# Four VectorE additions put ahead of ScalarE copies in the second MLP stage, with the order of all turns written anew

## The chip, the cores and the metric

The kernel runs on one core of a Trainium2 chip. The metric is the device time of one execution in microseconds (us). The core has five engines with queues of their own: PE (TensorE, matrix products, with its weight loads shown apart as PEld), DVE (VectorE), ACT (ScalarE), POOL (GpSimd) and SP (SyncE), which issues nearly all DMAs here. Each engine works through its own instructions in the order of the program and stops at the first one whose operands or buffers are not ready.

## The reference

```python
def _attn_ref(q, k, v, alpha):            # (B, H, S, D) = (4, 8, 768, 48)
    for t in range(S):
        state = alpha[:, :, t, :, None] * state + einsum('bhd,bhe->bhde', k[:, :, t], v[:, :, t])
        y[:, :, t] = einsum('bhd,bhde->bhe', q[:, :, t], state)

def _moe_ref(x, g_ln, w_ch1, w_ch2):      # x: (4, 768, 384), w_ch1: (384, 1536), w_ch2: (1536, 384)
    xn = (x - mean(x)) / sqrt(var(x) + 1e-06) * g_ln
    return x + maximum(xn @ w_ch1, 0.0) @ w_ch2
```

The output of the first function, its heads laid side by side, is the x of the second. The two weights arrive as float64 and are rounded to float32 inside the kernel.

## The kernel before

**Tiling.** The 768 positions are cut into six chunks of 128, and a unit of attention is one chunk of one of the four batches. Such a unit takes logarithms of alpha (L260), sums them with a triangular matrix (L474), scales q and k (L279), has them turned by DMA (L310, L313, L317; the first two chunks on TensorE, L295), forms scores (L490, masked by L343), the update of the state (L359, L372, L374), the output (L399), a layer norm and the transposed, normalised x (L463), which lands in the tile xT.

**MLP.** Chunk 0 uses plain products (L513, L525). Chunks 1 to 5 use a fast scheme with fewer products: x is combined by additions on VectorE (L775), fifteen hidden products (L801) are made for each of two groups of rows, their PSUM results are added up by VectorE, ScalarE and GpSimd (L809 to L844), relu runs on ScalarE (L852), the hidden values are combined on VectorE (L611), and twenty products (L624, `product`) give the output. In `product` each result `acc` lies in one PSUM bank and is added to one or two of the outputs `o(k)` (L634, L637) or kept: for n = 15, 11, 14 and 4 ScalarE copies it to e, f, g and q4 (L643, L648, L671, L684) and VectorE adds it to an output as well. `late` runs on GpSimd (L640).

**Buffers.** PSUM has eight banks in one ring (tag "bank"). Turned q and k, x combinations, hidden combinations and intermediate results share eleven SBUF tiles (tag "sum"). A new tile takes the one that was given back first, and its first writer waits for the last reader of the old content.

**Order.** Nothing is scheduled by a planner at build time. Each part of the work is a Python generator, a turn runs it to its next `yield`, and the string `ORDER` names the 1566 turns one by one. Lower case letters a to x are the 24 units of attention (a to d chunk 0, e to h chunk 1, and so on to u to x chunk 5); 0, 1, 2 and 3 are loads of alpha, k, q and v; 4 the sums of logarithms for two units, 5 the scores for two units; A to L rounding of the weights; Y, Z, P, Q the MLP of chunk 0; S and W weight combinations; X the combinations of x; M the products of chunks 1 to 5 (an even turn is a matrix product, the odd turn after it what is done with the result); V the hidden products of chunk 5; N the hidden combinations; R the relus; O reloads of x. Below, M190 is the turn of M with index 190, X22 the turn of X with index 22, and w0 the first turn of unit w; indices begin at 0. A turn's place is its index in `ORDER`. All instructions are issued in this order, each to the queue of its engine.

Of the kernel before, what the change touches and what calls it, by code (L numbers as in the profile page):

```python
# [20 lines left out]
STAGED = 3  # L21

ORDER = (
    "00aa00212b1cd2aab2b3cda1cabaadb0babb1aabbabBbccabccdedfacddaaaadd4acBfbbbb1dbbd2"
    "ecaAbff3ecffffdeeaeAee5bBdA0dgAccdhCdcdc1B4dYgYdYcccd2eCYYYYe3ghACggcgcghYhhhhdc"
    "ZBCf3ZZgfhZCeDDfe5fhYYD0YEZZ3eFEiYeZZY1gDYffjh2EYeYEFhfF4eFeffYgj0hjGigYYYjjYiiG"
    "ZgGZZhGjYiiZZZZHIjHYH3iHIj1SZZZZilZIZZkZSjJPh4ZgfjhgJiSiJ3g2SSgghKghgQSSSPlSSSSS"
    "SSeePKhYl5ISfKjjgjlkejSeShkSeklllPlfS3gLkjSSkkijLkLWQWWWWQQWifegffSSlgklfkihhhhh"
    "gejf0hjQj0iij31PQii23SPP5llnSkkii0PXXXiQMmX4Mmlk2XXXX1nlXMjkXlkMnniMM30MWMMMXMMM"
    "MMMMMMQMM2p1MnmOMRklMMnMmnWjoMMiMi4k3kmpllpnl0lW0mkmlpMMMmMMn1MMMWqMnMRjMMMRRRMM"  # L30
    "MMMMMMMm2MrRMmMMlMR2MMoj0ii5mnnkmmlORRnion3WmjRMMMlknMMROMWmknmNNNNmM4mkkkmlmNRM"
    "njNnpMMM11MMnlOo3j33MrMnkqlNNNNNN2MoNoMMMMpMoMMWMmoMMNXXnXMMNONXMqmmMMMMMMMMMMqX"
    "nXXXXqqoMMtMMmMXXMMnMppoMMMMMMMMMMMpRp0MnMMMMMMMMMMMq0vqM5pppoRooroqRrrpprrrM1OM"
    "MMMpMMpM1MRoMMoMMMRMoM2oMpqpMprMoMMrMMMsMMMMMROn5qrqR0RRmqqorrp4or3sMnMqq2rusorr"
    "RqRMMMprMtNRqOoNNNqNNotrmNMMMMMsssoNrMrMMNMMMNNpprNMMoppMMttMqMp0MMMnrsr2rrMNMNN"
    "3NM0tMt1MOMsw3MMXMXXXX1XMXMXMMqMXsMMMMtMM2tsXMMMMMMMMXMMMMMMMMMMMMMtRMMMM5tRttts"
    "4uMtxssMuMMMMRRMMMMvvq1ssquMMROMrMMMMMqussMRvuvM42sMttRtRtutM3tMtMMMqsMMRMMMMMMM"
    "sNtttMN3uOvxRtRNNNs1MNMRtMMMMMxONNNNssxqMMssNNMMvNMMMxsMMMMMMNMvNMxxNXMXXXXXOMMM"
    "MMMMMMXXXXx2XOwuMMMMMMMMMMMMMMMMMMMMMMMMMMRuvvRM3MMMRMRxM5uuuvuuvvwwwwwwMMRvOMMM"
    "MMMMMMMvMMvMxwuMwMuMvMMvMMMMMMMOuuvuRuRRvv5RxwxwxvvxwMMwMwRMNMMRRuMwvxwuxuNNNwxw"  # L40
    "wwxxwxNMwNxNNNvMMxxMMMMxNwNMMMMMMMMMMxXXMXXXXXXXXNMMXMMMVMVVVNVVVVVVVVVVVVVVVVVV"
    "VVVVVVVVVVVVVVVVVVVVVNVRRRRVVVONVVRVVRVVVVNVVVMVMMMMMOMMMMMMMVOORRRNNNNMMMMMMRRR"
    "NNNNNMMMMMNNNNMMMMMMMMMMMMMMMMMNNNMMMMMMMMMMMM"
)


# [1 line left out]
def kernel(  # L48
# [454 lines left out]
    def send(c, b, cols=slice(0, DM)):  # L503
        nc.sync.dma_start(out[b, c * P:(c + 1) * P, cols], ob_of[c, b][:, cols])
# [53 lines left out]
    def weights_ready():  # L558

        if "b" not in win:  # L560
            b = {(t, h): w2[:, t * NT:(t + 1) * NT, h * HM:(h + 1) * HM]
                 for t in range(3) for h in range(2)}
            win["b"] = {4: b[2, 0], 7: b[0, 1], 11: b[2, 0], 14: b[1, 0], 15: b[1, 0], 17: b[0, 0]}
        return win["b"]
# [23 lines left out]
    def blocks_of(c):  # L588
        if c not in win:
            win[c] = a = [third_of(c, t, b // HB)[:, :, b % HB] for b in range(B) for t in range(3)]  # L590
            win["a", c] = {1: a[10], 3: a[0], 4: a[8], 10: a[3], 14: a[7], 16: a[9], 17: a[6],
                           18: a[5]}
        return win[c], win["a", c]
# [23 lines left out]
    def product(c, n):  # L617
        if n == SECOND[0]:
            u = [work.tile([P, 512], FP32, name="u", tag="sum", bufs=11) for i in range(3)]
            win["u"] = [u[i // 2][:, i % 2 * HM:][:, :HM] for i in range(5)]  # L620
        acc = ps.tile([P, HM], FP32, name="ops", tag="bank", bufs=8)
        lhs, rhs = blocks_of(c)[1][n], weights_ready()[n]
        for j in range(NT):
            nc.tensor.matmul(acc, lhs[:, j], rhs[:, j], start=(j == 0), stop=(j == NT - 1))  # L624
        yield
        e, f, g, q4, r8 = win["u"]

        def o(k):
            return ob_of[c, k // 2][:, k % 2 * HM:][:, :HM]

        copy = nc.scalar.copy

        def add(x):
            nc.vector.tensor_add(x, acc, x)  # L634

        def sub(x):
            nc.vector.tensor_sub(x, x, acc)  # L637

        def late(x, y, op="add"):
            getattr(nc.gpsimd, f"tensor_{op}")(x, x, y)  # L640

        if n == 15:
            copy(out=e, in_=acc)  # L643
            add(o(0))
        elif n == 3:
            add(o(0))
        elif n == 11:
            copy(out=f, in_=acc)  # L648
            sub(o(0))
        elif n == 2:  # L650
            nc.vector.tensor_sub(f, acc, f)
        elif n == 18:
            sub(o(1))
            sub(o(3))
        elif n == 10:
            add(o(2))
        elif n == 19:
            sub(o(3))
            add(o(5))
        elif n == 0:  # L660
            add(e)
        elif n == 1:
            sub(o(1))
            sub(o(7))
        elif n == 6:
            sub(o(1))
            late(o(1), e)
            late(o(1), f)
            send(c, 0)
        elif n == 14:  # L670
            copy(out=g, in_=acc)  # L671
            add(o(4))
        elif n == 5:
            nc.vector.tensor_sub(g, acc, g)
            late(f, g)
        elif n == 9:
            sub(f)
            late(o(2), f)
            late(o(3), f)
            send(c, 1)  # L680
        elif n == 8:
            nc.vector.tensor_add(r8, acc, e)
        elif n == 4:
            copy(out=q4, in_=acc)  # L684
            add(o(4))
        elif n == 17:
            add(o(4))
        elif n == 12:
            sub(o(5))
            add(o(7))  # L690
        elif n == 13:
            add(q4)
            late(o(5), q4)
            late(o(5), g, "sub")
            late(r8, q4, "sub")
            late(o(7), r8)
            late(o(6), r8)
        elif n == 7:
            add(o(5))
            send(c, 2)  # L700
            send(c, 3, slice(HM, DM))
        else:
            add(o(6))
            send(c, 3, slice(0, HM))
        yield
# [154 lines left out]
    def mlp():  # L860
        for c in range(1, NCB):
            if c + 1 < NCB:
                yield from hidden_products(c)
            for n in SECOND:
                yield from product(c, n)
# [51 lines left out]
```

## Time and profile before

| | us |
|---|---|
| median of 3 runs (415.96 to 416.23) | 415.96 |
| the profiled execution | 415.94 |
| its span | 414.2 |
| PE busy (matrix products) | 401.8, 97% |
| PEld busy (weight loads) | 352.4, 85% |
| DVE busy | 325.0, 78% |
| ACT busy | 231.4, 56% |
| POOL busy | 159.4, 38% |

The granted clock of TensorE is full through the whole span. 1.7 us of the profiled execution lie outside its span. Views name an instruction by its line in the kernel and by its tiles (written<-read); the number in brackets at a row of the timeline is the idle time of the engine just before, with what ended it. SPq is SP's queue issuing a DMA; the time in such a row is the issue, not the transfer.

### The profile page before, as it was taken

How to read it: one execution, taken by the hardware profiler on the slowest of the kernel's cores; microseconds unless marked ns; L12 is line 12 of the kernel's file. 1: busy time of each engine (PE TensorE's matmuls, PEld its weight loads, DVE VectorE, ACT ScalarE, POOL GpSimd, SP SyncE). 2: the span in 40 equal slices, each digit the busy share in tenths (PEclk: the TensorE clock that was granted, in tenths of full speed). 3: DMA queues.
4: the chain of work that ended last, by engine and by line, in shares of the span. 5: the costliest groups of instructions: out<-in, count | busy, mean ns of one | idle time of the engine just before them, and what ended most of it. 6: DMA issues, size and time to landing. Idle time of an engine off the chain costs nothing.

```text
span 414.2 us, 11459 instructions
## 1 busy us (share of the span) xinstructions
PE 401.8 (97%) x4568; PEld 352.4 (85%) x4568; DVE 325.0 (78%) x622; ACT 231.4 (56%) x528; POOL 159.4 (38%) x180
## 2 busy tenths in 40 slices
PE   8979999999999999999999998999999999999996
PEld 6868878666578899988899977899988899889996
DVE  4599989999799799986688566779957677766764
ACT  6897468897158887337578113975125972142100
POOL 4250110001138660546731147641554700668214
PEclk9999999999999999999999999999999999999999
DMA  7979966989887968657765773464654742100301
GB/s 225 284 233 241 299 196 178 252 280 227 160 257 240 211 176 207 218 146 169 181 185 146 234 200 48 112 217 95 196 121 113 134 126 69 40 0 2 114 21 57
DMA packets 108061, 68.43 MB, mean 165 GB/s; under 512 B 73788, under 2 KB 100028, under 8 KB 108008
## 3 DMA queue, kind: packets, MB, share of 16 engines
q1 hardware_dynamic: 107976, 67.69, 61.1%
q8 instruction: 36, 0.59, 0.6%
q14 instruction: 17, 0.14, 0.1%
q0 software_dynamic: 32, 0.00, 0.0%
HBM read 34.29 MB, written 21.06 MB: 134 GB/s over the span
## 4 chain that ended last, share of the span: by engine, by line
PE 81%; DMA 5%; DVE 4%; SPq 3%; ACT 3%; POOL 2%; issue 1%; DVEq 0%; POOLq 0%; ACTq 0%
PE ops L624 30%; PE hps L801 28%; PE hps L513 6%; PE ops L525 6%; PE yps L399 4%; PE aps L490 2%; PE ups L359 2%; SPq L463 2%; DMA ra<-in_alpha_dram 2%; PE lps L474 1%; DMA rk<-in_k_dram 1%; DMA vn<-in_v_dram 1%; PE tps L295 1%; DMA turned<-sent 1%; PE yps L383 1%
## 5 line engine op out<-in xcount | busy, mean ns | idle before, releaser
L640 POOL TENSOR_TENSOR ob<-ob,u 128x192 f32<-128x192 f32 x40 | 26.2, 667 | 90.5 <-DVE ob L637 74.0
L801 PE MATMUL hps<-sum,w 128*128 128x256 f32 x192 | 46.9, 380 | 0.0
L852 ACT ACTIVATE hT<-hT 128x512 f32<-128x512 f32 x48 | 28.8, 624 | 23.7 <-POOL hT L823 17.8
L801 PEld LDWEIGHTS hps<-sum,w 128*128 128x128 f32 x192 | 36.3, 190 | 5.0
L624 PE MATMUL ops<-w,hT 128*128 128x192 f32 x224 | 39.8, 326 | 0.0
L374 POOL TENSOR_TENSOR mid<-mid,gate 112x192 f32<-112x192 f32 x20 | 11.4, 576 | 68.7 <-DMA gate<-row 22.4
L624 PEld LDWEIGHTS ops<-w,hT 128*128 128x128 f32 x224 | 37.0, 190 | 0.3
L801 PE MATMUL hps<-xT,w 128*128 128x256 f32 x136 | 34.6, 381 | 0.0
L513 PE MATMUL hps<-xT,w 128*128 128x256 f32 x144 | 32.6, 382 | 1.0 <-DVE mid L372 1.0
L310 ACT COPY planes<-qk 128x1024 uint16<-128x1024 uint16 x32 | 32.6, 1038 | 1.2 <-DVE qk L279 1.2
L525 PE MATMUL ops<-w,hT 128*128 128x384 f32 x96 | 32.2, 490 | 0.0
L513 PEld LDWEIGHTS hps<-xT,w 128*128 128x128 f32 x144 | 26.9, 190 | 5.7 <-DVE mid L372 1.1
L634 DVE TENSOR_TENSOR ob<-ops,ob 128x192 f32<-128x192 f32 x50 | 17.0, 350 | 15.5 <-PE ops L624 4.8
L801 PEld LDWEIGHTS hps<-xT,w 128*128 128x128 f32 x136 | 25.6, 190 | 4.1 <-DVE at L343 0.6
L624 PE MATMUL ops<-ws,sum 128*128 128x192 f32 x160 | 28.5, 326 | 0.0
L525 PEld LDWEIGHTS ops<-w,hT 128*128 128x128 f32 x96 | 17.9, 190 | 11.7
L624 PEld LDWEIGHTS ops<-ws,sum 128*128 128x128 f32 x160 | 26.4, 190 | 0.1
L260 ACT ACTIVATE la<-ra 128x384 f32<-128x384 f32 x24 | 12.2, 519 | 23.7 <-DMA ra<-in_alpha_dram 23.7
L624 PE MATMUL ops<-ws,hT 128*128 128x192 f32 x128 | 23.4, 326 | 0.0
L374 POOL TENSOR_TENSOR st<-st,gate 112x192 f32<-112x192 f32 x16 | 12.1, 765 | 25.7 <-DVE st L372 25.2
L624 PE MATMUL ops<-more,sum 128*128 128x192 f32 x120 | 22.0, 326 | 0.0
L624 PEld LDWEIGHTS ops<-ws,hT 128*128 128x128 f32 x128 | 21.3, 190 | 0.1
(253 smaller groups left out, 1096.4 us busy)
## 6 DMA issues: line engine op xcount, KB each, us to landing
ws<-in_moe_w_ch_dram SPq DMA_DIRECT2D x12, 768.0 KB
sent<-planes SPq DMA_DIRECT2D x32, 256.0 KB
vn<-in_v_dram SPq DMA_DIRECT2D x12, 384.0 KB
kept<-x SPq DMA_DIRECT2D x20, 192.0 KB
sentx<-parts SPq DMA_DIRECT2D x20, 192.0 KB
ob<-kept SPq DMA_DIRECT2D x20, 192.0 KB
out_dram<-ob SPq DMA_DIRECT2D x19, 192.0 KB
rq<-in_q_dram SPq DMA_DIRECT2D x16, 192.0 KB
```

What stands on the lines that cost most here:

```text
L260: nc.scalar.activation(out=la, in_=raws.pop(("a", c, b)), func=AFT.Ln)
L310: part(c)(out=planes, in_=natural.rearrange("t (d w) -> t w d", w=2))
L359: nc.tensor.matmul(up[h, p], qk_of(c, b)[ts, 1, p, i, :h.stop - h.start], vn[ts, i, p], start=True, stop=True)
L374: nc.gpsimd.tensor_mul(new, new, by)
L399: nc.tensor.matmul(yps[r][halves[s], i, p], of, by, start=not (odd and inner), stop=bool(inner or not odd), skip_group_check=bool(odd))
L513: nc.tensor.matmul(hps, w1[:, j // 2, f, j % 2 * P:][:, :P], xT_of[0][:, f, bs], start=(f == 0), stop=(f == NF - 1))
L525: nc.tensor.matmul(ops_of[b], hT_of[c][:, j, b], w2[:, j], start=(j == 0), stop=(j == NJ - 1))
L624: nc.tensor.matmul(acc, lhs[:, j], rhs[:, j], start=(j == 0), stop=(j == NT - 1))
L634: nc.vector.tensor_add(x, acc, x)
L640: getattr(nc.gpsimd, f"tensor_{op}")(x, x, y)
L801: nc.tensor.matmul(acc[:, i], w, b, start=True, stop=True)
L852: nc.scalar.activation(out=x, in_=x, func=AFT.Relu)
```

## The change

In `product` the order of two lines is turned in the branches for n = 15, 11, 14 and 4: VectorE's addition from `acc` is issued ahead of ScalarE's copy of `acc`, where before it came behind. Each branch runs once per chunk 1 to 5, so twenty pairs are turned. Besides, `ORDER` is another string with the same 1566 turns, each generator named equally often as before. Of the 382 turns with a matrix product, 188 have another rank among them, by 1.7 places in the mean over all.

Places in `ORDER` of the turns that are spoken of below:

| turn | what it is | before | after |
|---|---|---|---|
| B3 | last two rounding steps of a weight piece (L198, L200) | 121 | 83 |
| a20, b20 | xT of chunk 0, first two units (L452) | 97, 103 | 109, 108 |
| 5, index 0 | scores of e and f (L490) | 102 | 123 |
| Y0 | first hidden product of chunk 0 (L513) | 124 | 134 |
| 3, index 8 | load of v for the units k and l (L133) | 413 | 402 |
| g23, h24, e23, f24 | transposes of x of chunk 1 (L463) | 400, 405, 401, 403 | 416, 417, 420, 421 |
| 4, index 4; k12; l12 | sums of m and n; state updates of k and l | 443, 447, 446 | 388, 433, 440 |
| M0 | first hidden product of chunk 1 (L801) | 440 | 468 |
| w0 | logarithm for unit w (L260) | 972 | 1020 |
| M190, M191 | product n = 4 of chunk 2, its addition and copy | 974, 975 | 967, 968 |
| X22 to X29 | eight combinations of x of chunk 3 | 976 to 987 | 952 to 965 |
| t9, s9 | last DMA transposes of t and s (L317) | 1027, 1003 | 1038, 1064 |
| 5, index 7 | scores of s and t (L490) | 1033 | 1065 |
| M228, M252 | hidden products of chunk 3 | 1032, 1105 | 1033, 1062 |

```diff
--- before.py
+++ after.py
@@ -21,26 +21,26 @@
 STAGED = 3
 
 ORDER = (
-    "00aa00212b1cd2aab2b3cda1cabaadb0babb1aabbabBbccabccdedfacddaaaadd4acBfbbbb1dbbd2"
-    "ecaAbff3ecffffdeeaeAee5bBdA0dgAccdhCdcdc1B4dYgYdYcccd2eCYYYYe3ghACggcgcghYhhhhdc"
-    "ZBCf3ZZgfhZCeDDfe5fhYYD0YEZZ3eFEiYeZZY1gDYffjh2EYeYEFhfF4eFeffYgj0hjGigYYYjjYiiG"
-    "ZgGZZhGjYiiZZZZHIjHYH3iHIj1SZZZZilZIZZkZSjJPh4ZgfjhgJiSiJ3g2SSgghKghgQSSSPlSSSSS"
-    "SSeePKhYl5ISfKjjgjlkejSeShkSeklllPlfS3gLkjSSkkijLkLWQWWWWQQWifegffSSlgklfkihhhhh"
-    "gejf0hjQj0iij31PQii23SPP5llnSkkii0PXXXiQMmX4Mmlk2XXXX1nlXMjkXlkMnniMM30MWMMMXMMM"
-    "MMMMMMQMM2p1MnmOMRklMMnMmnWjoMMiMi4k3kmpllpnl0lW0mkmlpMMMmMMn1MMMWqMnMRjMMMRRRMM"
-    "MMMMMMMm2MrRMmMMlMR2MMoj0ii5mnnkmmlORRnion3WmjRMMMlknMMROMWmknmNNNNmM4mkkkmlmNRM"
-    "njNnpMMM11MMnlOo3j33MrMnkqlNNNNNN2MoNoMMMMpMoMMWMmoMMNXXnXMMNONXMqmmMMMMMMMMMMqX"
-    "nXXXXqqoMMtMMmMXXMMnMppoMMMMMMMMMMMpRp0MnMMMMMMMMMMMq0vqM5pppoRooroqRrrpprrrM1OM"
-    "MMMpMMpM1MRoMMoMMMRMoM2oMpqpMprMoMMrMMMsMMMMMROn5qrqR0RRmqqorrp4or3sMnMqq2rusorr"
-    "RqRMMMprMtNRqOoNNNqNNotrmNMMMMMsssoNrMrMMNMMMNNpprNMMoppMMttMqMp0MMMnrsr2rrMNMNN"
-    "3NM0tMt1MOMsw3MMXMXXXX1XMXMXMMqMXsMMMMtMM2tsXMMMMMMMMXMMMMMMMMMMMMMtRMMMM5tRttts"
-    "4uMtxssMuMMMMRRMMMMvvq1ssquMMROMrMMMMMqussMRvuvM42sMttRtRtutM3tMtMMMqsMMRMMMMMMM"
-    "sNtttMN3uOvxRtRNNNs1MNMRtMMMMMxONNNNssxqMMssNNMMvNMMMxsMMMMMMNMvNMxxNXMXXXXXOMMM"
-    "MMMMMMXXXXx2XOwuMMMMMMMMMMMMMMMMMMMMMMMMMMRuvvRM3MMMRMRxM5uuuvuuvvwwwwwwMMRvOMMM"
-    "MMMMMMMvMMvMxwuMwMuMvMMvMMMMMMMOuuvuRuRRvv5RxwxwxvvxwMMwMwRMNMMRRuMwvxwuxuNNNwxw"
-    "wwxxwxNMwNxNNNvMMxxMMMMxNwNMMMMMMMMMMxXXMXXXXXXXXNMMXMMMVMVVVNVVVVVVVVVVVVVVVVVV"
-    "VVVVVVVVVVVVVVVVVVVVVNVRRRRVVVONVVRVVRVVVVNVVVMVMMMMMOMMMMMMMVOORRRNNNNMMMMMMRRR"
-    "NNNNNMMMMMNNNNMMMMMMMMMMMMMMMMMNNNMMMMMMMMMMMM"
+    "0aa00bbc21021ca2bad1a0abaabdcdbbebaBaa3a2bb1ccfccbc4bccfBeaa01b2dBdacdaddgAdbhbb"
+    "3bbBeafaddf4febffdcefbaAahCebaedeAd2d3cdddA5ccgccd1C3eYfdfdc0eCYYYYCeYfYicggYYYe"
+    "cfAjhggggfB4efhef1ieeecfhDhEhhffDZ5CYZZZZDZ3ghFEZZZgYZjEZZDF2g0hhZGZghE3iFFikgYj"
+    "YgZGYiZilihijjHYYYhYYjhjGG4IhjHggZZggiHShjYIZZZkYZZYSSSSIiSSjZJQJhY32QSSSSSSIS5S"
+    "j1SijlJPjjSHejLPikegg0ghhSklQlkikkK0lik3LijlLlKlSiPPkKWQklnWmWiWWlg14feSeeeihghQ"
+    "fj3PShfh2ifff215ghnSefSkmiPlQkQiQkklSSnjlWinlOXnmmXX0XXjXnmm31XXmX0PMlkSWMMMMMXX"
+    "MMM21MMMMpM0MMMMnjljMMMkMMRMMMlWMo4mmklpllllMllpPWnknMM3MmMMMMkMp0MMMMMWMMMMRRMn"
+    "irMMMMRR3R3M2MOMoMMM0M5nmWnRRmnmnpMmmOlMkopRkMMq02nR1MNOkmMMkMM4mnkkRNijjjjmNNNN"
+    "jntnmoo1MWMMMMMiNkNollMMNMMmWRNsq2mMNNoio3MpMj0MpN0MnMMNMMMqNMrMXqMXMMMMqNMqMMnn"
+    "MqXXXXXX3XqMMMpMMMMMMoMMMMMMMXMMMMMXMMMMMMMMMMovnMpO5noo3Rp4poOrrourMrrMMooMr1MM"
+    "MMMMMMRRoORRRMMMMpotMpMpmMptMMMMMqqrnsoMprMooRMMMRpppm5r2rrqRq1ppqqMqooRRoMoNNpM"
+    "NNMMMrrMMp1mqmrtMOp2prqMmo4rNsqqNMNNRrnnrntNNMNp2MMMMMM3NMtMMMMsN1MMMMNNXMMNMXXX"
+    "MXsXXXMMMMMMMrXXsr00OMuuMMMqt3MMMMMMMMMsMXtMMMMOMMMMMMMMMrMMwM2tMqvurrrrMMMssMtM"
+    "MMMMRMMMqMMMMMMMMMMMMMMqs5sstsxsstttqtMRMMsMMuRtvRRRRROM4uuu3tssRNsNtMRttstRwsMN"
+    "MtqNMMMtN3svRMtOxqNvvsMNNNtMMMMt2NN3MMsMMNMMMMMMst1usNMMNvvMMNMMxxMMMNXXXXXMMXXX"
+    "XMMMMMM2MMMMMMXMMMMxxMXMMMMMMMMvuMMMMMMvMMMMM1M5vuRvRRuxvwwOvxuwwxwuwOMMMMMvMMMM"
+    "MuMMvRMRuwMMMMMxMw3MMMvvMuMMMuuuRMu5xwxxvuvRwwMxwwRMuMvvRMMMMRxwvRvRNNxwxuwNNwxN"
+    "vwwNNNNNNOxxxxxwOxNwNxMMMMMMMMMMMMMMMMMMwMMXXXXXXMOXXXXNMVMMMMVNNVVXVVVVVVVVVVVM"
+    "VVVVVVVVVVVVVVVVVVVVVVVVVVVVVVVVVRRRRRVVVVVVVVVVVMMRMVMMRRORRRMMMMMNNNNNNNMMNRMN"
+    "NNOMMMMMMONNMMMMMMMMMMMMMMMMMNNNMMMMMMMMMMMMMM"
 )
 
 
@@ -640,13 +640,13 @@
             getattr(nc.gpsimd, f"tensor_{op}")(x, x, y)
 
         if n == 15:
+            add(o(0))
             copy(out=e, in_=acc)
-            add(o(0))
         elif n == 3:
             add(o(0))
         elif n == 11:
+            sub(o(0))
             copy(out=f, in_=acc)
-            sub(o(0))
         elif n == 2:
             nc.vector.tensor_sub(f, acc, f)
         elif n == 18:
@@ -668,8 +668,8 @@
             late(o(1), f)
             send(c, 0)
         elif n == 14:
+            add(o(4))
             copy(out=g, in_=acc)
-            add(o(4))
         elif n == 5:
             nc.vector.tensor_sub(g, acc, g)
             late(f, g)
@@ -681,8 +681,8 @@
         elif n == 8:
             nc.vector.tensor_add(r8, acc, e)
         elif n == 4:
+            add(o(4))
             copy(out=q4, in_=acc)
-            add(o(4))
         elif n == 17:
             add(o(4))
         elif n == 12:
```

## The prediction

> **What bounds the kernel now.** The page first: the span, and the busy time of each engine.
>
> ```profile
> span 414.2 us, 11459 instructions
> PE 401.8 (97%) x4568; PEld 352.4 (85%) x4568; DVE 325.0 (78%) x622; ACT 231.4 (56%) x528; POOL 159.4 (38%) x180
> ```
>
> PE is idle for 414.2 − 401.8 = 12.4 us and no other engine is near full. The change adds and removes no instruction, so PE's 401.8 us stay as long as the clock stays, and all that can move is the 12.4 us. Where they lie is read from the windows by stage (columns: length, busy time and instructions of PE, PEld, DVE, ACT, POOL, granted clock, DMA share, GB/s).
>
> ```profile
> 0.00:30.38 30.38, 26.72 (x410) 21.26 (x410) 20.06 (x44) 25.25 (x59) 12.32 (x24) 1.00 0.80 244
> 30.38:111.54 81.16, 80.05 (x1050) 59.84 (x1046) 75.63 (x122) 57.12 (x128) 8.39 (x13) 1.00 0.88 231
> 111.54:116.28 4.74, 3.12 (x78) 2.00 (x77) 3.58 (x10) 3.19 (x10) 0.00 (x0) 1.00 0.87 271
> 116.28:235.00 118.72, 118.08 (x1461) 108.37 (x1461) 97.47 (x190) 75.47 (x174) 57.37 (x59) 1.00 0.73 192
> 235.00:256.37 21.37, 19.24 (x215) 16.33 (x213) 14.60 (x30) 4.96 (x13) 11.86 (x12) 1.00 0.67 164
> 256.37:411.00 154.63, 154.60 (x1364) 144.60 (x1364) 113.33 (x228) 65.39 (x149) 69.42 (x74) 1.00 0.35 92
> 411.00:414.24 3.24, 0.00 (x0) 0.00 (x0) 0.36 (x1) 0.00 (x0) 0.00 (x0) 1.00 0.35 121
> ```
>
> Length less PE busy gives the idle time: 3.7 in the opening, 1.1, then 1.6 in under five microseconds at the first product of chunk 1 (I call this the junction), 0.6, 2.1 around 235 to 256, nothing in the long last stretch, and a tail of 3.2 (the last output leaving), which the change doesn't touch. The clock is full in all of them. So there are three places to work out: opening, junction, and the stretch from 235 us, which I call the late place. PE's waits name what ends them (total, times, longest):
>
> ```profile
> PE xps L449 <- DVE xn L438: 1.1, 1, 1.1
> PE hps L513 <- DVE mid L372: 1.0, 1, 1.0
> ```
>
> The one of 1.1 lies in the opening, that of 1.0 at 54 us; the others of over 0.6 us stand in brackets in the timeline rows below.
>
> **The four swaps.** DVE waits for the copies in two large pieces:
>
> ```profile
> DVE ob L634 <- ACT u L684: 4.1, 1, 4.1
> DVE ob L634 <- ACT u L671: 2.5, 1, 2.5
> L684 ACT COPY u<-ops 128x192 f32<-128x192 f32 x5 | 1.6, 316 | 32.6 <-PE ops L624 32.6
> ```
>
> Copy and addition only read `acc`, yet the later one in the program waits for the earlier. Turned round, the addition waits for PE alone and ACT's copy waits for the addition. For a pair in which both engines are free this shifts the same two reads about: the addition may begin up to 316 ns earlier (row L684) and the copy later by the length of an addition, some 0.35 us. In itself that is nothing, since DVE is busy 78% and ACT 56% while PE works through eight banks ahead of them. It counts only where ACT is stuck when its copy comes up, and there the late place stands.
>
> **Late place.** The timeline:
>
> ```profile
> 235.30 0.52 ACT L260 ACTIVATE la<-ra 128x384 f32<-128x384 f32 x1 [7.25 <-DMA ra<-in_alpha_dram]
> 235.73 0.30 ACT L684 COPY u<-ops 128x192 f32<-128x192 f32 x1
> 236.06 0.36 DVE L634 TENSOR_TENSOR ob<-ops,ob 128x192 f32<-128x192 f32 x1 [4.13 <-ACT u L684]
> 239.45 1.13 PE L801 MATMUL hps<-sum,ra 128*128 128x256 f32 x4 [0.81 <-DVE sum L775]
> 245.19 6.05 SPq L317 DMA_TRANSPOSE turned<-sent  x3
> 246.70 1.24 SPq L317 DMA_TRANSPOSE turned<-sent  x1
> 247.61 2.75 PE L801 MATMUL hps<-sum,w 128*128 128x256 f32 x12
> 252.59 0.69 DVE L833 TENSOR_TENSOR hT<-hps,hT 128x512 f32<-128x512 f32 x1 [2.23 <-POOL hT L827]
> 253.65 1.10 PE L490 MATMUL aps<-turned 48*64 48x64 f32 x59 [1.30 <-DVE hT L833]
> ```
>
> The first four rows are a chain: ACT stands 7.25 us at w0, whose alpha has not landed; the copy of n = 4 (M191) is queued behind it; DVE's addition waits 4.13 us for the copy, with X22 and the other combinations of x queued behind; PE runs out of combined x and waits 0.81 us. After the change three things break it: the addition is ahead of the copy, w0 stands at place 1020 instead of 972, and X22 to X29 (eight additions of about 0.42 us, 3.4 us in all) stand ahead of M190. Any one would do, so I take the 0.81 as gone.
>
> The 1.30 us at 253.65 belong to the scores of s and t (turn 5, index 7). They are put down to DVE's L833, but that ends at 253.28 while the scores read what the DMA transposes `turned` bring, whose issue ends, in the row of three, at 245.19 + 6.05 = 251.24; start at 253.65 is 2.4 us after that. A transpose at the junction behaves alike (below: issued until 107.29 + 2.52 = 109.81, its reader starts 2.6 us later at 112.40). So the wait is a landing. After the change the scores stand 12 hidden products later; a product is four instructions of L801, 2.75 / 3 = 0.92 us by the row of twelve, so that is 11 us, far more than 1.3. But the last transposes, s9, stand at place 1064, directly ahead of the scores at 1065. Their buffer of the ring is read until M242, five products = 4.6 us ahead of the scores, while one issue (1.24) and the landing (2.4) take 3.6. That leaves 1.0 us: no wait at best, and if SP needs as long for it as for the row of three, 6.05 + 2.4 − 4.6 = 3.9. I take 0.6, the length of one or two short issues more than the margin covers; it is nearer to the row of one. Late place: −0.81 − 1.30 + 0.6 = **−1.5** (−2.1 to +1.8).
>
> **Junction.**
>
> ```profile
> 107.29 2.52 SPq L463 DMA_TRANSPOSE xT<-sentx  x1
> 109.86 1.23 SPq L120 DMA_DIRECT2D ra<-in_alpha_dram  x2
> 111.13 0.59 SPq L133 DMA_DIRECT2D vn<-in_v_dram  x1
> 111.82 0.41 SPq L116 DMA_DIRECT2D rk<-in_k_dram  x1
> 112.40 0.76 DVE L775 TENSOR_TENSOR sum<-xT 128x256 f32<-128x256 f32 x2 [2.11 <-DMA xT<-sentx]
> 112.47 1.10 PE L801 MATMUL hps<-xT,extra 128*128 128x256 f32 x4 [0.93 <-issue]
> 113.62 0.88 PE L474 MATMUL lps<-la,consts 64*64 64x384 f32 x8
> 114.91 0.42 DVE L775 TENSOR_TENSOR sum<-sum,xT 128x256 f32<-128x256 f32 x1
> 115.14 1.14 PE L359 MATMUL ups<-vn,qk 64*64 64x48 f32 x64 [0.65 <-DMA vn<-in_v_dram]
> 116.21 1.13 PE L801 MATMUL hps<-sum,ra 128*128 128x256 f32 x4
> ```
>
> M0 waits 0.93 us for the last transposed x of chunk 1 (DVE's first addition starts at 112.40 with the same landing), then k12 and l12 wait 0.65 for v. Sum 1.58. After the change the v load stands ahead of the four transposes (place 402, they at 416 to 421), and the sums (0.88) and state updates (1.14) stand ahead of M0: 2.0 us of work that covers the landing. Both waits go. What is late next is M2, which needs X0 to X6; these take DVE from 112.40 to 114.91 + 0.42 = 115.33. PE would be there at 116.21 − 1.58 = 114.6, so 0.7 us come back if the transposes land as before.
>
> They may land later. Six loads (two L120 together 1.23, L133 0.59, L116 0.41 and three more like it) now stand ahead of the last transpose on SP, 3.5 us of issue. Where SP was waiting for turned units anyhow, loads moved up fill idle time; if it had none, the landing is at 112.40 + 3.5 = 115.9, X6 ends 2.9 later with M2 at about 118.4, which is 2.2 us behind its present 116.21 and means a wait of 3.8. SP's issue ahead of 109.86 depends on `sentx`, made by other engines, so I take 0.7: **−0.9** (−1.6 to +2.2).
>
> **Opening.**
>
> ```profile
> 25.56 1.16 PE L490 MATMUL aps<-qT,kT 48*64 48x64 f32 x64 [0.76 <-ACT kT L300]
> 26.40 0.55 DVE L452 TENSOR_TENSOR xT<-xps,small 128x384 f32<-128x384 f32 x1
> 30.38 0.92 PE L513 MATMUL hps<-xT,w 128*128 128x256 f32 x3
> L198 DVE SCALAR_TENSOR_TENSOR ws<-ws 128x768 int32<-128x768 int32 x12 | 11.8, 980 | 1.4 <-ACT ws L196 1.3
> L200 DVE SCALAR_TENSOR_TENSOR w<-w,ws 128x768 f32<-128x768 f32 x12 | 12.1, 1006 | 0.4
> L196 ACT ACTIVATE ws<-ws,small 128x768 int32<-128x768 int32 x12 | 12.3, 1027 | 3.1 <-DVE ws L194 2.0 <-ACT hT L516 0.9
> L271 ACT ACTIVATE lps<-lps 128x384 f32<-128x384 f32 x24 | 11.8, 490 | 0.0
> ```
>
> B3 moves ahead of the xT of a20 and b20: 980 + 1006 ns = 2.0 us more DVE work before them. The last of these ends at 26.95 and Y0 starts at 30.38, a margin of 3.4 us that falls to 1.4, so it costs nothing; without that cover it would be 2.0. On ACT, ahead of the copies that the first scores (turn 5, index 0) read, stand in addition one L196 (1.03), two L260 (0.52 each, as at 235.30) and a pair L270, L271 (0.98): 3.05 us. The scores move from 25.56 to 28.6; their turn is moved back from place 102 to 123 to match, with Y0 ten places later. With the same work ahead of it, Y0 comes between 30.3 and, if the two engines' delays don't hide behind each other, about 32. I take **+0.3** (−0.5 to +1.7: half of the wait of 1.1 saved, or Y0 at 32). The wait of 1.0 near 55 us I leave.
>
> **All other places.** 188 of 382 matrix turns change rank in stretches that now show 0.6 us idle in 118.72. Some sums are made much earlier in the order (4, index 4: 443 to 388) and hold a PSUM bank longer. There is nearly nothing to gain here and something to lose: **+0.3** (0 to 1.5).
>
> **Sum.** −1.5 − 0.9 + 0.3 + 0.3 = −1.8 from the profiled execution's 415.94 (span 414.2 and 1.7 outside it), which is the median's 415.96 to the second digit: 414.1.
>
> **Rivals.**
>
> *SP's queue is the late one (slower).* One mechanism: loads put ahead of DMA transposes on SP delay the landing of turned data. At the junction the wait is 3.8 instead of 0.7 (+3.1); at the late place the scores keep their 1.3 instead of 0.6 (+0.7): 414.1 + 3.8 = 417.9. It decides once the moved-up loads find less than about 3 of their 3.5 us as idle time of SP. For it: DMA shares of 0.88 and 0.87 in the two windows there, the highest of the kernel. Against: the last transpose's source is made by other engines, and while SP waits for it the loads cost nothing. Chance 0.30.
>
> *The wait is only turned round (no difference).* ACT's copy now waits for the addition, and the copy of n = 4 is itself an operand of a later addition. If DVE is behind at such a place, ACT and then relu and layer norm behind it wait, and half of the 0.81 comes back (+0.4); with other places at +1.1 instead of 0.3 this is 414.1 + 0.4 + 0.8 = 415.3. The trace speaks half for it: the 4.13 us are a wait between two readers. The Trainium skill ("PSUM — Partial Sum Buffer", section "PSUM bank collisions raise a hardware error") says that any two engines at one bank and quadrant collide, two readers included, so that their accesses must be ordered; by that rule the swap cannot remove the wait, only reverse it, and the sum would be 415.3. The 4.13 us between two readers agree with the ordering. Chance 0.16.
>
> *More goes than I count.* The scores of s and t wait for nothing (−0.6), M2 neither (−0.7), and half of the 1.0 or the 1.1 in the first 55 us goes, with nothing lost elsewhere: about 412.2. Chance 0.07.
>
> **How the numbers follow.** The forecast, 414.1, has 0.47, its own range 413.0 to 415.1. Faster is forecast and gain case, 0.47 + 0.07 = 0.54; same is the turned wait, 0.16 (0.2% is 0.83 us, about what a measurement of this kernel can tell from no change); slower is SP's queue, 0.30. The range reaches from the gain case's 412.2 to SP's 417.9, which leaves out the outer halves of these two, less than 2 in 10.
>
> **What would show it.** Right: no DVE addition L634 waiting over 2 us for L684; no PE wait for `sum` near 235 us; the junction's idle time below 1 us with the wait now at M2; the scores of s and t waiting below 1 us; PE busy still 401.8. Wrong: an L801 at the start of chunk 1 waiting 2 us or more behind `sum` or `xT` (SP's queue); the opening's idle time above 5 us; several new waits of 0.5 us between 116 and 235 us or behind 256 us, in particular for banks that ACT's late copies hold.

## The result, and the profile after

The changed kernel takes 421.17 us (median of 4 runs, 420.04 to 422.76) against 416.1 us for the kernel before in the same call: a ratio of 1.012, 95% interval 1.0083 to 1.0156. It is slower by 5 us; 414.1 had been forecast, with a range up to 417.9. The profiled execution took 422.76 us. Runs of different calls come from different chips, so times below are compared by their ratio to the kernel before in the same call.

The page of the changed kernel, span and engines:

```profile
span 421.0 us, 11454 instructions
PE 405.5 (96%) x4568; PEld 355.7 (85%) x4568; DVE 326.7 (78%) x622; ACT 230.2 (55%) x528; POOL 159.1 (38%) x180
```

The span grew by 6.8 us: TensorE's idle time by 3.1 (12.4 to 15.5), and, which no term of the prediction allowed for, its busy time by 3.7 with the same 4568 instructions. The windows by stage, cut as in the prediction (Y0 starts at 33.73, M2 at 121.75; the columns are as before, with the granted clock behind POOL; the tail of 3.2 us is as before and left out):

```profile
0.00:33.73 33.73, 28.19 (x411) 23.09 (x411) 21.64 (x45) 26.05 (x63) 11.40 (x24) 0.95 0.87 259
33.73:113.00 79.27, 79.27 (x1077) 59.12 (x1077) 72.97 (x117) 58.39 (x136) 11.31 (x13) 1.00 0.82 228
113.00:121.75 8.75, 4.38 (x48) 2.79 (x46) 6.67 (x16) 3.91 (x5) 0.12 (x1) 1.00 0.95 191
121.75:126.05 4.30, 4.30 (x12) 3.53 (x13) 3.88 (x7) 0.59 (x1) 1.19 (x2) 0.60 0.88 271
126.05:240.00 113.95, 112.07 (x1429) 101.92 (x1428) 91.33 (x182) 66.51 (x154) 53.01 (x55) 1.00 0.68 172
240.00:261.00 21.00, 21.00 (x110) 19.36 (x109) 15.30 (x31) 9.75 (x23) 12.07 (x14) 1.00 0.56 163
261.00:417.80 156.80, 156.31 (x1489) 145.93 (x1487) 114.51 (x230) 64.98 (x147) 70.00 (x75) 1.00 0.40 98
```

| TensorE idle (last row: lost), us | before | after | change | forecast |
|---|---|---|---|---|
| start to junction | 3.7 + 1.1 | 5.5 + 0.0 | +0.8 | +0.3 |
| junction | 1.6 | 4.4 | +2.7 | -0.9 |
| M2 to 240 us | 0.6 | 1.9 | +1.2 | +0.3, with the row "behind it" |
| late place | 2.1 | 0.0 | -2.1 | -1.5 |
| behind it | 0.0 | 0.5 | +0.5 | |
| lost clock: 5% of 33.73 and 40% of 4.30 | 0 | 3.4 | +3.4 | none |

The late place is as clean as the better end of its range. The loss is the junction, and two stretches in which the granted clock is half. TensorE's waits name the operands:

```profile
PE hps L801 <- DVE sum L775: 4.6, 2, 4.2
PE ups L359 <- DMA vn<-in_v_dram: 2.3, 1, 2.3
```

The timeline of the junction (SP's issue, DVE, PE):

```profile
108.31 6.71 SPq L463 DMA_TRANSPOSE xT<-sentx  x4
...
117.73 0.43 DVE L775 TENSOR_TENSOR sum<-xT 128x256 f32<-128x256 f32 x1 [1.94 <-DMA xT<-sentx]
118.08 0.55 DVE L279 TENSOR_TENSOR qk<-rk,lps 128x384 f32<-128x384 f32 x1
118.54 0.55 DVE L279 TENSOR_TENSOR qk<-rq,eq 128x384 f32<-128x384 f32 x1
119.01 0.42 DVE L775 TENSOR_TENSOR sum<-xT 128x256 f32<-128x256 f32 x1
...
121.75 0.46 PE L801 MATMUL hps<-sum,ra 128*128 128x256 f32 x1 [4.16 <-DVE sum L775]
```

The four transposes of chunk 1's x stand in one row on SP and end at 115.02 (before: 109.81). The x lands at 117.73 (before: 112.40). VectorE then scales unit m between X0 and X1, 0.93 us, and M2 waits 4.16 us for X6.

What x itself waited for stands in the chain of work that ended last (first two rows: start, length, and what it was) and in SP's own waits (third row):

```profile
105.67 5.25 DMA sentx<-parts
113.74 3.97 DMA xT<-sentx
SPq L463 <- DMA sentx<-parts: 1.1, 1, 1.1
```

The writings of x to `sentx` are issued late and close together. They stand behind four transposes of `turned`, where before they alternated with them, from 94.07 on (those rows are shown in "SP's queue by itself" below):

```profile
97.53 5.44 SPq L317 DMA_TRANSPOSE turned<-sent  x4
104.12 0.95 SPq L461 DMA_DIRECT2D sentx<-parts  x2
```

The third writing, issued at 105.67, takes 5.25 us to land, and 1.1 us of the row of 6.71 is SP waiting for it. SP's row of issues that leads up to this begins 3.3 us later than before (91.83 instead of 88.58, the first writing of `planes`) and is 2.0 us longer from there to the end of the last transpose (23.2 instead of 21.2).

What the clock did is seen when the time is cut into the stretches in which it was granted (3.41 us each):

```profile
13.41:16.82 3.41, 1.54 (x24) 1.00 (x16) 0.93 (x3) 2.32 (x6) 1.22 (x2) 1.00 0.95 289
16.82:20.23 3.41, 2.87 (x56) 2.90 (x58) 2.74 (x5) 1.01 (x1) 0.00 (x0) 0.50 0.68 210
115.80:119.21 3.41, 1.78 (x7) 0.95 (x5) 1.48 (x4) 0.55 (x1) 0.00 (x0) 1.00 1.03 208
119.21:122.63 3.42, 0.89 (x4) 0.84 (x5) 3.25 (x9) 1.92 (x3) 1.00 (x2) 1.00 0.70 149
122.63:126.05 3.42, 3.42 (x10) 2.73 (x9) 3.04 (x5) 0.59 (x1) 0.31 (x1) 0.50 0.95 306
```

A stretch in which TensorE idles 1.87 us (3.41 - 1.54) or 2.53 us is followed by one at 0.50; the stretch with 1.63 us idle was not. Each costs up to 1.7 us, half its length. The Trainium skill ("TensorE: Matmul & The Clock Gate", section "Part 1: The HAM clock gate (the "warmup" mystery)") has a free-running window of 3413 ns, which these stretches agree with; it drops the clock after a whole idle window, and here half of one was enough.

### The profile page after: what moved, and what is told of

Its sections match the earlier page's. It is cut to its first block, busy times and chain, and to the rows that moved or that the text cites. A ratio compares the mean times of both kernels' runs of the same rounds, so it can differ in the third digit from the quotient of the medians.

```text
span 421.0 us, 11454 instructions
## 1 busy us (share of the span) xinstructions
PE 405.5 (96%) x4568; PEld 355.7 (85%) x4568; DVE 326.7 (78%) x622; ACT 230.2 (55%) x528; POOL 159.1 (38%) x180
## 4 chain that ended last, share of the span: by engine, by line
PE 77%; DMA 7%; ACT 7%; DVE 4%; SPq 2%; issue 2%; POOL 1%; ACTq 0%; POOLq 0%; DVEq 0%
PE hps L801 30%; PE ops L624 29%; PE hps L513 8%; PE yps L399 4%; DMA sentx<-parts 2%; PE ups L359 2%; PE aps L490 2%; DMA vn<-in_v_dram 2%; DVE sum L775 1%; PE ops L525 1%; PE lps L474 1%; DMA xT<-sentx 1%; DMA ra<-in_alpha_dram 1%; DMA kept<-x 1%; ACT xn L432 1%
## 5 line engine op out<-in xcount | busy, mean ns | idle before, releaser
L801 PE MATMUL hps<-sum,w 128*128 128x256 f32 x192 | 47.9, 385 | 0.0
L801 PEld LDWEIGHTS hps<-sum,w 128*128 128x128 f32 x192 | 36.9, 193 | 5.2
L801 PE MATMUL hps<-xT,w 128*128 128x256 f32 x136 | 34.6, 381 | 0.0
L513 PE MATMUL hps<-xT,w 128*128 128x256 f32 x144 | 32.7, 382 | 0.3 <-DVE w L200 0.3
L513 PEld LDWEIGHTS hps<-xT,w 128*128 128x128 f32 x144 | 26.8, 190 | 4.0 <-PE yps L383 0.4
L801 PEld LDWEIGHTS hps<-xT,w 128*128 128x128 f32 x136 | 25.6, 190 | 3.5
L685 ACT COPY u<-ops 128x192 f32<-128x192 f32 x5 | 1.6, 319 | 44.6 <-DVE ob L634 44.6
L820 POOL TENSOR_TENSOR hT<-hT,u 128x512 f32<-128x512 f32 x8 | 10.3, 1289 | 35.6 <-DVE u L819 35.6
L624 PEld LDWEIGHTS ops<-ws,hT 128*128 128x128 f32 x128 | 21.2, 190 | 0.0
```

Of the source, the lines that this page charges most:

```text
L513: nc.tensor.matmul(hps, w1[:, j // 2, f, j % 2 * P:][:, :P], xT_of[0][:, f, bs], start=(f == 0), stop=(f == NF - 1))
L801: nc.tensor.matmul(acc[:, i], w, b, start=True, stop=True)
L820: add_late(c4, c4, u2)
```

## Experiments

Turns are moved in `ORDER` and named as in the change; all kernels have the swaps unless it is said otherwise.

**Swaps alone, order alone.**

```diff
 swaps_alone: ORDER of before
-            copy(out=q4, in_=acc)
             add(o(4))
+            copy(out=q4, in_=acc)        (and n = 15, 11, 14)
 order_alone: ORDER of after, copies ahead of additions as in before
```

> The order of the turns of before, with the four additions ahead of the copies. Theory A (the loss comes from the new order, in two places at the front of the kernel: 2.3 us of waiting for v in the opening, 4.2 us at the first products of chunk 1, and after each a stretch of half clock): no loss here; VectorE's addition of n = 4 no longer waits 4.1 us for ScalarE, the 0.8 us wait of TensorE at 239 us goes, 415.2 us. Rival B (the loss comes from the swaps: ScalarE's copies now wait for VectorE and hold PSUM banks longer): 418 us or more, with TensorE waits spread over all five chunks. Rival C (the swap only turns the wait round): 415.9 to 416.3, no change.

> The new order with the copies ahead of the additions, as in before. Theory A: as slow as the changed kernel, 420 to 422.5 us, with the waits of 2.3 us for v and 4.2 us for combined x, and two stretches of half clock. Rival B: 416.5 or less.

Measured: swaps alone 0.9981 (0.996 to 1.0003), 415.93 us; order alone 1.0124 (1.0093 to 1.0155), 422.37 us. The order carries the whole loss (A); rival B is out. The waits of swaps_alone show what the swap does:

```profile
ACT u L685 <- DVE ob L634: 33.9, 4, 9.4
DVE u L634 <- ACT u L685: 2.0, 4, 0.8
```

ScalarE's copy of n = 4 now waits 33.9 us for the addition; before, it waited 32.6 for TensorE (row L684 in the prediction), so this is nearly no new wait. A later addition waits for the copy, 2.0 us in all where before VectorE waited 4.1 and 2.5. TensorE's wait near 239 us is gone from this trace. The gain, 0.2%, is at the edge of what these runs resolve: by time alone theory A and rival C can't be told apart. Order alone has the same wait at M2:

```profile
PE hps L801 <- DVE sum L775: 4.4, 2, 4.2
```

**The opening.**

```diff
 v_first: order of after
-  B0 (weight load)  ...  3 index 0 (load of v)
+  3 index 0  B0
 after_opening:     after up to Y0, then all other turns as in before
 before_opening:    before up to Y0, then all other turns as in after
 before_then_after: before up to M16, then all other turns as in after
```

> The changed kernel with one turn moved: the first load of v is issued ahead of the first load of a weight piece, not behind it. Theory A: TensorE's wait of 2.3 us for v at 17 us goes, and with it the half clock of one window of 3.4 us (1.7 us): 417 to 418 us; the wait and the half clock at chunk 1 stay. Rival D (all loads of the opening share the same full DMA engines, what one gains another loses): less than 1 us gained, 420.3 or more, with a new wait of TensorE for what the weight piece feeds or for other loads before 35 us.

> The new order up to Y0, the first product of the MLP, then the order of before for all other turns; with the swaps. The theory now (A2: the new opening loses 2 to 3 us by a late load and a window of half clock behind the wait; the first products of chunk 1 lose 4.2 us of waiting and 1.7 us or more of half clock; the rest gains about 1.4): TensorE reaches Y0 late, the late start is not made up, 418 to 420 us, with one wait of over 1.3 us before 30 us. Rival E (a late start is absorbed at the first products of chunk 1, where TensorE waits for other engines anyhow): 416 to 417 us, with the idle time near 112 us shorter than before's 1.6.

> The order of before up to Y0, then the new order; with the swaps. A2: the half clock and the wait in the opening go, the wait of 4.2 us at the first products of chunk 1 stays with its half clock: 418 to 419.5 us. Rival E: the wait at chunk 1 grows by what the opening gains, 420.5 us or more.

> The order of before up to the turn M16 (the first products of chunk 1), then the new order for all that is left; with the swaps. Theory A: the opening and the first products as in before, no half clock; from there on the waits that the changed kernel shows behind 135 us (0.7, 0.7, 0.5, 0.4) in place of before's (0.4, 0.2, 0.8, 1.3): 415.5 us, within 414.5 and 416.3. Rival B: 418 us or more.

Measured: v_first 1.0143 (1.011 to 1.0175), after_opening 0.9986 (0.9951 to 1.0021), before_opening 1.0128 (1.0088 to 1.0168), before_then_after 1.0118 (1.0059 to 1.0177). With v loaded first nothing is gained, and TensorE waits for what another load feeds instead, as rival D said:

```profile
PE tps L295 <- DVE more L279: 2.7, 1, 2.7
```

The new opening in front of the old order costs nothing that these runs resolve, and the old opening in front of the new order saves nothing: theory A2 fell for the opening. Rival E had the times nearly right, but in before_opening the wait at M2 grows only to 4.52 us, and its trace has a stretch of half clock in the old opening too, near 25 us. The wait for v is not the same in every run of the new opening either: 2.34 us in the changed kernel's profile, 1.45 in order_alone, 0.50 in filled. In after_opening Y0 starts 1.2 us later than in before (31.55 to 30.38), yet VectorE gets x at the same time as in before (112.40):

```profile
112.36 0.76 DVE L775 TENSOR_TENSOR sum<-xT 128x256 f32<-128x256 f32 x2 [1.35 <-DMA xT<-sentx]
```

In before_then_after no wait for x is left at the junction; the splice made a wait of its own (3.2 us at 127 us for a logarithm, whose alpha is loaded late there, and half clock behind it), so its time does not answer for what lies behind M16.

**The junction, step by step.**

```diff
 combos_first: order of after
-  X0 ... m2 m3 X1 ... m4 m5 ... X6
+  X0 X1 ... X6 m2 m3 m4 m5 m6
 norm_early: order of after
+  h19 g21 e19 e20 e21 g22 e22 ... h23 g23 e23     (g21 to e22 were at 386 to 397, g23 at 416, e23 at 420)
 norm_early_combos_first: both
 act_only: order of after
+  f23 n0 m0 4(index 4) i18                        (were 378, 380, 388, 409)
 act_sp_dve: act_only, combos_first, and
+  f24 2(index 9) 1(index 9)                       (loads, were 413, 414)
```

> The changed kernel with the scaling of unit m (VectorE's two multiplications L279 between X0 and X1, 0.93 us, and the copies and DMAs that follow from it) moved behind X6. A2 with VectorE as part of the cause: the combination X6 ends 0.9 us earlier, TensorE's wait of 4.2 us at M2 becomes 3.2; the share of the idle time in a window of 3.41 us decides on the half clock; 419 to 420.5 us. Rival S (SP's queue alone): the wait stays at 4.0 or more and the time at 421.

> The changed kernel with eight turns moved: the last steps of the layer norm of e and g (ScalarE) and the writing of their x come ahead of ScalarE's copies for k and l, as in before, and their two transposes ahead of f's writing. Theory L (x of chunk 1 lands late because ScalarE works on units k, l, m, n ahead of the layer norms, and because all four transposes stand behind the last writing): two transposes leave SP earlier, the last one lands about 3.5 us earlier, TensorE's wait at M2 falls from 4.2 to 1 us or less and the half clock goes: 415 to 417 us. Rival Q (SP's other loads set it): the wait stays over 3 us, 419 us or more.

> The same, and the scaling of unit m behind X6. Theory L: another 0.9 us at most, as far as a wait at M2 is left; 414 to 416 us, at or below before, with before's wait of 1.3 us near 252 us gone. Rival Q: 418 us or more.

> The changed kernel with four turns moved behind the last writing of chunk 1's x (f23): the logarithms of m and n, the sums that read them, and a copy for unit i; 1.7 us of ScalarE's work less ahead of the last layer norm, as in before. Theory L2 (ScalarE, busy without a break from 89 us on in the new order, ends the layer norms of chunk 1 late): x lands 1.7 us earlier relative to Y0, TensorE's wait at M2 falls from 4.2 to about 2.5 us, often without half clock; 418 to 420 us. Rival Q2 (the transposes are held by SP's own row of issues): x lands at most 0.5 us earlier, wait 3.7 or more.

> The same, two loads for unit m (1.0 us of SP's issue) moved behind the last transpose, and the scaling of m, which they feed, behind X6. If each engine adds its own part (ScalarE 1.7, SP 1.0, VectorE 0.9 us), the wait at M2 falls by 3.6 to under 1 us, no half clock: 415.5 to 417.5 us. Q2: 419 or more.

| | ratio to before | 95% interval | wait at M2 |
|---|---|---|---|
| combos_first | 1.0039 | 1.0007 to 1.0071 | 2.9 us |
| norm_early | 1.011 | 1.0064 to 1.0156 | 3.6 |
| norm_early_combos_first | 1.0105 | 1.0074 to 1.0135 | 2.6 |
| act_only | 1.0119 | 1.0081 to 1.0157 | 4.2 |
| act_sp_dve | 1.0114 | 1.0079 to 1.0149 | 3.7 |

With the combinations first the wait fell by 1.3 us, somewhat more than the 0.93 that was moved (1.0 between norm_early and norm_early_combos_first); three of its ten runs had no half clock at all, and it is the only one of these that is clearly nearer to before. The others missed. Pulling e's and g's steps forward let their two transposes leave earlier, while f's writing then stood behind them on SP; besides, M0 itself waits 1.0 and 1.1 us for x in the two norm_early kernels, which the column does not show.

In act_only, 1.7 us less of ScalarE's work left the wait where it was, and theory L2 fell. Rows of ScalarE show why a single engine's relief does nothing (first the changed kernel, then act_only; `parts` is what the writing reads):

```profile
105.58 0.83 ACT L458 COPY parts<-xn 128x768 uint16<-128x768 uint16 x1
104.26 0.83 ACT L458 COPY parts<-xn 128x768 uint16<-128x768 uint16 x1
```

The last `parts` is ready 1.3 us earlier, but its writing is issued at 106.73 instead of 106.70: SP's own row gets there no sooner. In act_sp_dve the two loads that were moved had stood in time in which SP would have waited anyhow: its row of four transposes takes 7.8 us instead of 6.7, of which 2.3 are waits for `sentx`.

One more kernel, loads_behind (1.0188, 1.0131 to 1.0246), moved three loads for m and n (1.4 us of issue) behind the last transposes, and the scaling of m and n behind X6; 417 to 418 us had been expected. A later load into the same tile then comes ahead of n's scaling, so n is scaled with other data, and TensorE waits 4.7 us for that scaling; its time is no answer. But chunk 1's x does not depend on that scaling, so SP's waits up to 116 us can be read:

```profile
SPq L463 <- DMA sentx<-parts: 2.1, 2, 1.1
```

With the loads out of the way SP waits 2.1 us for the landing of `sentx` instead of 1.1, and from the start of SP's row x lands 0.9 us earlier (25.0 us after 92.03, against 25.9 after 91.83 in the changed kernel). In both runs the chain that ended last goes through the landing of the third writing, and not through loads behind it: these stand, for the most part, in time in which SP waits.

**SP's queue by itself.**

```diff
 loads_ahead: order and copies of before
+  0(index 8) 0(index 9) 3(index 8) 1(index 8) 2(index 8) e22
```

> The kernel before (copies first) with five loads (two of alpha, v, k, q; 3.2 us of SP's issue) moved ahead of the writing and the transposes of chunk 1's x, where the new order has them. Theory Q2 (SP's queue alone is enough): x lands 2 to 3 us later, TensorE waits 2 to 3 us more at chunk 1's first products: 418 to 420 us, in some runs with half clock. Theory P: SP has 3 to 4 us of idle time there, the loads fill it, x lands at most 1 us later: 416 to 417.5.

Measured: 1.0059 (1.0037 to 1.0082), 418.67 against 416.18 us, +2.5 us; Q2 holds in time and landing. SP's timeline in this run:

```profile
94.09 0.66 SPq L116 DMA_DIRECT2D ra<-in_alpha_dram  x1
94.81 1.13 SPq L120 DMA_DIRECT2D ra<-in_alpha_dram  x2
96.03 0.53 SPq L133 DMA_DIRECT2D vn<-in_v_dram  x1
96.66 0.41 SPq L116 DMA_DIRECT2D rk<-in_k_dram  x1
97.17 0.38 SPq L116 DMA_DIRECT2D rq<-in_q_dram  x1
...
106.39 6.20 SPq L463 DMA_TRANSPOSE xT<-sentx  x4
```

The last transpose ends at 112.59 instead of 109.81 and VectorE gets x at 114.91 instead of 112.40. TensorE waits 1.89 us at M0 (0.93 before) and 0.90 at scores at 107.67 (none before), a little less than the 2 to 3 us more of Q2; a stretch of half clock follows at 115.39 in this execution. Ahead of the writings of x the loads found no idle time. The kernel before says why, in rows that the prediction did not add up (the last of them, 107.29, stands in the prediction):

```profile
94.07 0.66 SPq L461 DMA_DIRECT2D sentx<-parts  x1
94.78 1.29 SPq L317 DMA_TRANSPOSE turned<-sent  x1
96.17 0.52 SPq L461 DMA_DIRECT2D sentx<-parts  x1
96.80 2.62 SPq L317 DMA_TRANSPOSE turned<-sent  x2
99.48 1.11 SPq L461 DMA_DIRECT2D sentx<-parts  x1
100.68 1.28 SPq L317 DMA_TRANSPOSE turned<-sent  x1
102.05 0.53 SPq L461 DMA_DIRECT2D sentx<-parts  x1
102.67 3.90 SPq L463 DMA_TRANSPOSE xT<-sentx  x3
106.62 0.58 SPq L116 DMA_DIRECT2D ra<-in_alpha_dram  x1
```

With the 2.52 of 107.29, SP is occupied for 15.0 of the 15.7 us up to 109.81. The run shows what such loads cost in the order of before; in the new order they stand at other places among the writings.

**The middle in its old order.**

```diff
 middle_as_before: order of after, its turns from k2 to M0 sorted as in before (M0 stays at 468)
 middle_wide:      order of after, its turns from Y0 to M0 sorted as in before
```

> The changed kernel with its own 131 turns between k2 and M0 put in the order that they have in before; opening, M0 and all behind it stay new. Theory P (nothing single is to blame: in the new order f23, the last writing of chunk 1's x, stands behind 5.0 us more of SP's issues, 4.8 us more of ScalarE's work and 7.6 us more of TensorE's than in before, so only 8.5 us of TensorE's work lie between it and M0 instead of 14.1, while its x needs some 10 us to land): x lands before TensorE is at M2, no wait there, no half clock: 414.5 to 416.5 us. Rival Z (the loss is in the new order's opening or behind M0 and shows at M2 only because that is where engines meet): 419 or more.

> The same for the 333 turns between Y0 and M0. Theory P: as middle_as_before within 1 us. If the order between Y0 and k2 counts too, this one is faster by over 1 us.

Measured: 1.0261 (1.0231 to 1.0291) and 1.0194 (1.0148 to 1.024), far off. The x side of theory P held in middle_wide, the time did not:

```profile
112.08 0.76 DVE L775 TENSOR_TENSOR sum<-xT 128x256 f32<-128x256 f32 x2 [2.59 <-DMA xT<-sentx]
PE lps L474 <- ACT la L260: 2.4, 1, 2.4
```

x lands as in before and M2 waits for no `sum`. But M0 keeps its new place behind the sums of m and n and the state updates, and these now wait for alpha and v, loaded late again (2.4 us here, 3.9 in middle_as_before), with half clock behind it. In these two kernels the new place of M0 would need early loads, and early loads ahead of the writings of x delay it (loads_ahead).

**The clock.**

```diff
 filled, filled_half: order of after; in hidden_product for M2, ahead of its products
+            for _ in range(16):          (8 in filled_half)
+                nc.tensor.matmul(acc[:, 0], idle[:, :P], idle[:, :2 * P], start=True, stop=True)
```

> The changed kernel with sixteen matrix products of 256 columns added in front of M2's, into M2's own bank, which M2 then overwrites: 3.5 us of work for TensorE at full clock that needs no x and changes no result. Theory H (a window of 3.41 us in which TensorE idles about half the time or more is followed by a window at half clock): the wait of 4.2 us is filled, no half clock near 120 us, M2 starts no later than before: 1.7 us faster than the changed kernel in a run with one such window less, 3.4 with two less; 418 to 420 us on this chip. Rival N (the clock falls for another reason): the half clock stays, same time or slower.

> The changed kernel with eight added products in front of M2 instead of sixteen: in the run with sixteen they took 7.1 us, 0.44 each, and pushed M2 2.9 us behind its operand, so eight take 3.5 us and fit into the wait of 4.2. Theory H (half clock follows a window with about half of it idle): granted clock 1.0 near 120 us and M2 on time, 2.8 us faster than with sixteen and 1.7 to 3.4 faster than the changed kernel: 418.5 to 419.8 us. Rival N: 421 or more.

Measured: filled 1.0122 (1.0071 to 1.0174), filled_half 1.0089 (1.0058 to 1.012). Windows of filled:

```profile
114.60:121.50 6.90, 6.90 (x33) 6.07 (x33) 6.46 (x13) 2.48 (x3) 1.37 (x2) 1.00 0.87 226
```

The clock stayed full: five of six runs of filled and four of six of filled_half have a mean granted clock of 1.0, where every listed run of the changed kernel and of order_alone and v_first lies at 0.996 or less. At the junction H is right on the cause. A mean of 1.0 says that the opening was at full clock too, which the added products can't have done: TensorE waited only 0.50 and 1.41 us for v in these two profiles. In time the products were too long with sixteen (7.1 us, twice the 3.5 expected, M2 2.9 us behind its operand) and the gain with eight, 0.3% at overlapping intervals, is not settled; M2 still waits 1.47 us there. So the runs show what takes the clock down, and not that the time comes back with it.

**The gains without the loss.**

```diff
 swaps_scores_later: swaps, order of before
-  5(index 7) t10 ... M229 ... M230 ... M231 M232
+  M229 M230 M231 M232 5(index 7) t10 ...
```

> The order of before with the four swaps, and the scores of s and t two hidden products later (two products, 1.8 us). Theory A: the wait of 0.8 us for combined x near 239 us is gone by the swap, and the wait of 0.8 to 1.4 us in front of these scores is filled; 0.8 to 1.3 us faster than before in the same call, a ratio of 0.997 to 0.998. Rival: what is gained there is lost at the scores' followers (VectorE's masking, the state update), no difference.

Measured: 0.9973 (0.9946 to 1.0001), 415.66 against 417.03 us. Its waits of TensorE:

```profile
PE lps L474 <- DVE hT L844: 0.8, 1, 0.8
PE hps L801 <- DVE sum L775: 0.3, 1, 0.3
```

The wait in front of the scores is gone and one of 0.8 us stands two products on, ahead of the next sums: part is given back. It has the lowest ratio of all kernels here, but its interval reaches 1 and overlaps with that of swaps_alone: a gain of 0.3% is likely and not shown.

## Why the prediction was wrong

**The step that failed is the junction's term of 0.7 us for M2's wait: it lets x of chunk 1 land as before, at 112.40, because SP's transposes depend on `sentx`, "made by other engines".** x landed at 117.73, and the wait measured 4.16. The dependence was read rightly; that `sentx` would be written as early as before was taken for granted. Its last writing was issued at 106.70 instead of 102.05. Of the 5.2 us by which the last transpose ends later, 3.3 are there when SP's row begins (a late start for which the sum had no term), and the row is 2.0 us longer: three turns of loads with 2.2 us of issue (1.17 + 0.53 + 0.46), behind the transposes in before, now stand ahead of the third writing, and SP waits 1.1 us for that writing to land, while other issues of the row take less.

**"Loads moved up fill idle time" was half right.** It fails ahead of the writings of x: in the order of before SP is occupied for 15.0 of 15.7 us there, which was there to read, and five loads cost 2.5 us (loads_ahead). It holds, for the most part, behind them, where SP waits for `sentx` (loads_behind).

**VectorE's part was left out.** Multiplications of unit m stand between X0 and X1. While X6 is what TensorE waits for, their 0.93 us count in full (combos_first: wait 1.3 us shorter).

**The rival's 3.8 us for this wait is near the 4.16 by luck.** Its sum has a slip: 115.9 and 2.9 make 118.8, not 118.4, so by its own terms the wait is 4.2 and its time 418.3. And the terms were others: x landed 5.3 us later and not 3.5, VectorE added 0.93, and TensorE came to M2 3.0 us later itself (ready at 117.59, not 114.6), which hides as much of the wait: 0.7 + 5.3 + 0.9 − 3.0 is 3.9.

**A term was missing: the clock.** The prediction held the clock full "in all of them". Two windows of half clock cost 3.4 us. The rival's 417.9 + 3.4 is 421.3, beside a median of 421.17; that too is luck, for its 0.7 at the scores did not come and 1.7 us of small waits behind M2 came in its place.

**The opening** was judged by VectorE's and ScalarE's work alone; the load of v, behind a weight load of 768 KB, was not looked at, and TensorE waited 2.3 us for it (0.5 to 1.5 in other runs of the same opening). The term, +0.3, measured +0.8 and a window of half clock. By after_opening, whose profile has no half clock, the opening alone does not move the end.

**Right:** the swaps (nothing in themselves, the wait of 4.13 us dissolved), the two waits of the late place (-2.1 for -1.5), and TensorE's work as such. The rival by which the wait is only turned round describes what ScalarE does (its copy of n = 4 waits 33.9 us for VectorE in swaps_alone), but not a loss: it had waited 32.6 us for TensorE before. The rule of the Trainium skill that it rests on ("PSUM — Partial Sum Buffer", section "PSUM bank collisions raise a hardware error") agrees with the trace: the copy, now the second reader, waits for the first. A time of 415.3 did not follow from it.

**Open:** why SP's row begins 3.3 us later. It begins with ScalarE's `planes`, which wait 2.6 us for VectorE's scaling (L279) at 90.76. The late opening alone does not explain it: with the old opening (before_opening) the row begins at 92.05 all the same. No run put x back to its old time in the new order with all else in place, so the parts of the late landing are read from traces and not shown one by one. The waits of 0.4 to 0.7 us behind M2 were not traced either.

## What to carry to other kernels

Before a load is moved ahead on a DMA-issuing queue, add up what that queue issues ahead of the next thing that somebody waits for; "it waits anyway" is a number to be read, not a reason. Where the queue waits for another engine, place that engine's work in the new order too: here the writings of x came 10 us later at their start. Where an order is changed in many places, look for the operand that the busiest engine reaches next with the least slack: two gains of 1 us at other places are lost to one late landing. And price an idle stretch of TensorE of about 2 us or more at up to twice the 1.7 us that the clock behind it can cost.

## What was not expected of the hardware

The granted clock moves in stretches of 3.41 us, and a stretch in which TensorE idles for about half (1.87 and 2.53 us here) is followed by one at half clock; in order_alone and v_first two such stretches stand in a row (6.8 us at half clock, near 120 us). There is no sharp bound in idle time: 1.63 us in a stretch of the changed kernel did not do it, while in norm_early, where the other half of the stretch held small products of the scores and the state, 1.55 us did:

```profile
13.56:16.97 3.41, 1.86 (x34) 1.28 (x27) 1.90 (x4) 2.59 (x7) 1.22 (x2) 1.00 0.96 281
16.97:20.38 3.41, 3.41 (x64) 3.32 (x61) 1.78 (x4) 1.37 (x2) 0.00 (x0) 0.50 0.81 246
```

The same kernel meets the raster differently from run to run: the changed kernel had mean clocks of 0.991 to 0.996, and its run at 0.996 was its fastest, 420.04 us. The kernel before is not free of it: in one call 8 of its 25 runs lie at 0.991 to 0.996.

A timeline row that joins several issues holds the waits between them as well. The four transposes of 6.71 us in the changed kernel are 5.5 us of issue and 1.1 of waiting for `sentx`; single ones of chunk 1 took 1.2 to 2.5 us.
